# Attention's outputs kept as features by tokens in an adaLN transformer block

## The chip, the cores and the metric

The kernel runs on one core of a Trainium2 chip. A core has five engines with a queue each, which work through their instructions in order and wait for each other by semaphores: TensorE (PE in the profile, with its weight loads as PEld), VectorE (DVE), ScalarE (ACT), GpSimd (POOL) and SyncE (SP), which here only issues DMAs. The metric is the device time of one execution in microseconds (us), the median of several runs.

## The reference

An adaLN block over 2048 tokens of 576 features: 32 heads of 18 features, full softmax attention, then a gated layer of width 4608.

```python
h = layernorm(x) * (1 + ca) + sa
q, k, v = split(h @ wqkv)                      # 32 heads of 18
o = softmax(q @ k.T * 18**-0.5) @ v            # per head
x = x + ga * (o @ wo)
h = layernorm(x) * (1 + cb) + sb
x = x + gb * ((sigmoid(h @ w_gate) * (h @ w_up)) @ w_down)
```

The six vectors sa, ca, ga, sb, cb and gb come from silu(c) @ w_mod. Everything is float32; many products are taken as sums of high and low parts.

## The kernel before

The program first normalizes x and projects q, k and v, which go to DRAM split in high and low parts (qd, kd) or stay in SBUF (vaug). Then comes attention, and then the gated layer as a long row of products in which PE is filled to the brim.

Attention runs over 32 units: two halves of 1024 queries, and in each 16 pairs of heads. A unit has 16 steps kt, one for each 128 keys. A step does four score products (L1084: 128 keys by 512 queries, two heads by two blocks c of 512), four exponentials on ACT (L1088) and, two steps behind, the products of the exponentials with the values (L656). These add up over the unit in one PSUM tile `o` of 128 rows, in which head h and block c take the rows from 32 (2 h + c): 18 rows of outputs, features by queries, and below them a row of the exponentials' sums. Beside this each step computes a part of the row maxima for the units ahead (L550 on PE, L556, L559 and L561 on DVE and ACT).

The order on PE and ACT is written out by hand. A table `STEPS` has a line of words for each kind of pair of steps: `t` is a score product with its exponential, `m`, `r` and `x` a product for the maxima, `V` the values of a step, `A` and `B` their halves, `K` calls taken(), `G` asks the generator rows0 or rows1 for its next piece, and `c` moves every piece of work in the list `follow` one step on. A piece that ends with "g" makes the next pair of steps a heavy one, with the order "full"; the others take "half", "rows" (units 15 to 27) or a line of their own for kt 0, 2, 4 and 12. DVE, POOL and SP are ordered by a scheduler; an instruction given to paced() also waits for the exponential written last. bank() hands out seven PSUM banks in turn to the score products, the maxima and everything else in attention.

At a unit's start load_heads(u + 2) has SP issue eight loads of q and k (L514 to L522, 1512 KB). Where a unit's maxima are complete, spread() turns them and SP issues four small DMAs from mrows into the q tile (L590), about at kt 12.

A unit's end, before: taken() copies `o` to oT in SBUF (L673, at kt 1 of the next unit). At kt 2, outputs() turns oT back to tokens by features with four transposes on PE (L683), ACT copies the result (L699), DVE takes the reciprocals of the sums (L702), GpSimd scales (L705) into Os[half], 1024 tokens by 576 features in SBUF. The projection by wo then works row tile by row tile (project_o): three or four transposes of a row tile (L772), one more for the last 64 features in the first half (L789), copies on DVE (L774 to L790), splits on GpSimd, and two groups of products (L805). Row tiles 0 to 7 run in units 16 to 20, row tiles 8 to 15 in units 27 to 31 over the first 384 features only; the other 192 features go through DRAM (oend) and are added in last_rows(), during the gated layer, again with transposes (16).

Of the kernel before, what the change touches and what calls it, by code (L numbers as in the profile page):

```python
# [23 lines left out]
P = 128  # L24
# [63 lines left out]
def tile_block(ctx, tc, x_in, wqkv, wo, w_gate, w_up, w_down, c_in, w_mod, out):  # L88
# [206 lines left out]
    oend = dram.tile([P, 8, D - DL], F32, name="oend")  # L295
# [338 lines left out]
    Os = [Oa]  # L634
# [33 lines left out]
    def taken():  # L668

        if "whole" in state:  # L670
            half, p, acc = state.pop("whole")
            oT = epool.tile([P, 512], F32, name="oT")
            nc.scalar.copy(oT, acc)  # L673
            state["end"] = (half, p, oT)

    def outputs():

        if "end" not in state:
            return
        half, p, oT = state.pop("end")  # L680
        tp = bank().rearrange("p (b q) -> p b q", q=P)
        for b in range(4):
            nc.tensor.transpose(tp[:, b, :], oT[:, b * P : (b + 1) * P], ident)  # L683

        yield
        tq = tp.rearrange("p b (j e) -> p j b e", e=32)
        rec = epool.tile([P, 4, 4], F32, name="rec")
        if half == 1 and p == H // 2 - 1:
            nc.vector.reciprocal(rec, tq[:, :, :, DH])
            state["last"] = epool.tile([P, 512], F32, name="oT")[:, 0 : 16 * DH].rearrange("p (t e) -> p t e", t=8)  # L690
            for h in range(2):
                nc.vector.tensor_tensor(
                    state["last"][:, :, h * DH : (h + 1) * DH].rearrange("p (c b) e -> p c b e", c=2),
                    tq[:, 2 * h : 2 * h + 2, :, 0:DH],
                    rec[:, 2 * h : 2 * h + 2, :].unsqueeze(3).to_broadcast([P, 2, 4, DH]),
                    op=ALU.mult,
                )
            return
        nc.scalar.copy(oT, tp.rearrange("p b q -> p (b q)"))  # L699
        yield  # L700
        tq = oT.rearrange("p (b j e) -> p j b e", j=4, e=32)
        nc.vector.reciprocal(rec, tq[:, :, :, DH])  # L702
        for h in range(2):
            f0 = (2 * p + h) * DH
            nc.gpsimd.tensor_tensor(  # L705
                Os[half][:, :, f0 : f0 + DH].rearrange("p (c b) e -> p c b e", c=2),
                tq[:, 2 * h : 2 * h + 2, :, 0:DH],
                rec[:, 2 * h : 2 * h + 2, :].unsqueeze(3).to_broadcast([P, 2, 4, DH]),
                op=ALU.mult,
            )  # L710


# [4 lines left out]
    def load_wo():  # L717
# [31 lines left out]
        for _ in range(4):  # L749
            yield  # L750
# [3 lines left out]
    def project_o(t):  # L754

        wo_h, wo_l, we = weights
        if t <= 8:
            held_rows[:] = temp([P, 2048], F32R), temp([P, 2048], F32)
        T, T_ = held_rows
        if t < 8:  # L760
            xt, full, od = T_[:, 0:D], T_[:, 1024:1536], T_[:, 1536:1664]
        else:
            T, T_ = T[:, 1024 * (t % 2) : 1024 * (t % 2) + 1024], T_[:, 960 * (t % 2) : 960 * (t % 2) + 960]
            xt, full = T_[:, 0:D], T_[:, D : D + 384]
        nc.gpsimd.dma_start(xt, x_rows[:, t, :])
        src = Os[t // 8][:, t % 8, :]
        n = 4 if t < 8 else DL // P
        oh = T[:, 0 : n * P]
        ol = T[:, 512 : 512 + n * P]
        pt = bank()  # L770
        for i in range(n):
            nc.tensor.transpose(pt[:, i * P : (i + 1) * P], src[:, i * P : (i + 1) * P], ident)  # L772
# [1045 lines left out]
```

## Time and profile before

| what | value |
|---|---|
| median of 3 runs | 2798.32 us (2797.94 to 2798.35) |
| the profiled execution: its time, its span | 2804.88 us, 2803.1 us |
| mean granted clock of TensorE | 0.998 |
| busy: PE, DVE, ACT, POOL | 2771.9, 2306.3, 1609.3, 814.6 us |
| attention | from about 236 to 1533 us |
| a unit without projection work | 38.3 us |

The profile is one execution. Its page gives busy times of the engines, the chain of work that ended last, groups of equal instructions (a count, the mean time of one, and what the engine waited for before it) and the DMA issues; the trace behind it can be asked for a stretch of time or one engine. A row of a timeline has start, length, engine, source line, operation and tiles, and in brackets the idle time before it and who ended that. Matmuls overlap, so the distance between starts tells more than the length of one.

### The profile page before, as it was taken

Reading aid. Unit: us, or ns where it says so; the run is one execution under the profiler, and the core shown is the slowest. Engines: PE = TensorE matmul, PEld = TensorE weight load, DVE = VectorE, ACT = ScalarE, POOL = GpSimd, SP = SyncE. Lnnn points to the kernel's source line nnn. Section 1 sums busy time; section 2 is a strip of 40 time slices with the busy share of each in tenths; the row PEclk is TensorE's granted clock in tenths of the full one; section 3 lists DMA queues with packets and bytes.
Section 4 is the critical chain, followed back from the end, with each engine's and each line's share of the span. In section 5 each row is a group of like instructions: output and inputs, shape, how many; then the busy total and the mean of one; then the engine's idle time right before and its main releaser. Section 6 shows DMA issues by size and latency. Waiting matters only on the chain.

```text
span 2803.1 us, 50644 instructions
## 1 busy us (share of the span) xinstructions
PE 2771.9 (99%) x18637; PEld 1847.4 (66%) x18637; DVE 2306.3 (82%) x4370; ACT 1609.3 (57%) x3051; POOL 814.6 (29%) x1077
## 2 busy tenths in 40 slices
PE   7999999999999999999999999999999999999999
PEld 5975444444444444444444888888888888888888
DVE  7278999999998888999883778888898677777777
ACT  3215999999999878999888332333333222222221
POOL 3125207888843111663103222232221100000000
PEclk9999999999999999999999999999999999999999
DMA  5344224444432120232127766667767956566653
GB/s 172 121 157 140 78 61 162 171 169 166 172 133 82 36 58 24 98 106 71 43 68 227 273 222 223 240 213 273 278 245 280 339 195 201 194 200 195 200 195 120
DMA packets 170777, 462.59 MB, mean 165 GB/s; under 512 B 21212, under 2 KB 88032, under 8 KB 160416
## 3 DMA queue, kind: packets, MB, share of 16 engines
q1 hardware_dynamic: 150064, 360.72, 38.4%
q0 software_dynamic: 20464, 98.62, 9.9%
q8 instruction: 147, 2.41, 0.4%
q14 instruction: 102, 0.84, 0.1%
HBM read 281.92 MB, written 176.82 MB: 164 GB/s over the span
## 4 chain that ended last, share of the span: by engine, by line
PE 92%; DVE 4%; DMA 2%; issue 2%; POOL 0%; ACT 0%; SPq 0%; DVEq 0%; ACTq 0%; POOLq 0%
PE x L1225 26%; PE o L656 19%; PE s L1084 12%; PE s L550 11%; PE d L1375 8%; PE d L1307 6%; PE s L336 4%; PE s L805 2%; PE s L389 1%; DMA out_dram<-Oa 1%; DVE mx L556 1%; PE s L683 1%; DMA wq_raw<-in_A_wqkv_dram 1%; DVE w L1215 0%; DVE Oa L1379 0%
## 5 line engine op out<-in xcount | busy, mean ns | idle before, releaser
L1088 ACT ACTIVATE p<-s 128x512 f32<-128x512 f32 x2048 | 1069.1, 616 | 89.2 <-PE s L1084 62.6
L556 DVE TENSOR_REDUCE mx<-s 128x1 f32<-128x512 f32 x1568 | 1000.9, 683 | 101.3 <-PE s L550 75.1
L656 PE MATMUL o<-p,vaug 128*32 128x256 f32 (+1 forms) x5848 | 595.1, 478 | 0.1
L550 PE MATMUL s<-k,q 54*128 54x512 f32 x1920 | 548.6, 434 | 2.0 <-DVE t L775 1.0
L1084 PE MATMUL s<-q,k 56*128 56x512 f32 x1920 | 527.7, 440 | 0.0
L550 PEld LDWEIGHTS s<-k,q 54*128 54x128 f32 x1920 | 273.4, 184 | 231.9 <-DVE mx L561 88.0
L1084 PEld LDWEIGHTS s<-q,k 56*128 56x128 f32 x1920 | 249.8, 184 | 232.1 <-ACT p L1088 72.9
L1225 PE MATMUL x<-k,w 128*128 128x512 f32 x1512 | 370.0, 392 | 0.0
L1225 PEld LDWEIGHTS x<-k,w 128*128 128x128 f32 x1512 | 276.8, 188 | 53.3 <-PE o L656 0.8
L1375 PE MATMUL d<-wd,hh 128*128 128x288 f32 x1248 | 249.9, 295 | 2.4 <-DVE Oa L1379 2.4
L656 PEld LDWEIGHTS o<-p,vaug 128*32 128x32 f32 x5848 | 116.2, 108 | 203.1 <-issue 187.5
L1225 PE MATMUL x<-big,w 128*128 128x512 f32 x1008 | 245.5, 392 | 0.7 <-DVE u L1724 0.7
L1225 PE MATMUL x<-w,w 128*128 128x512 f32 x1008 | 245.3, 391 | 0.0
L1225 PEld LDWEIGHTS x<-big,w 128*128 128x128 f32 x1008 | 185.1, 188 | 37.0 <-DVE u L1724 1.1
L1225 PEld LDWEIGHTS x<-w,w 128*128 128x128 f32 x1008 | 184.3, 188 | 34.5
L1375 PEld LDWEIGHTS d<-wd,hh 128*128 128x128 f32 x1248 | 202.2, 188 | 6.2 <-DVE Oa L1379 3.1
L1375 PE MATMUL d<-wd,hl 128*128 128x288 f32 x624 | 184.3, 295 | 0.0
L1379 DVE TENSOR_TENSOR Oa<-Oa,d 128x288 f32<-128x288 f32 x312 | 136.6, 453 | 55.1 <-PE d L1375 51.2
L561 DVE CUSTOM_DVE_ANT_0 over<-s,over 128x512 f32<-128x512 f32 x240 | 163.9, 683 | 1.3 <-PE s L1084 1.2
L559 ACT ACTIVATE over<-s 128x512 f32<-128x512 f32 x240 | 145.8, 608 | 11.3 <-PE s L550 9.3
L1234 ACT ACTIVATE sg<-x 128x512 f32<-128x512 f32 x36 | 21.6, 599 | 210.2 <-PE x L1225 210.2
L1206 ACT CAST w<-S 128x768 fp32r<-128x768 f32 x71 | 59.4, 836 | 137.8 <-POOL S L1179 136.0
(275 smaller groups left out, 3898.5 us busy)
## 6 DMA issues: line engine op xcount, KB each, us to landing
ws<-w SPq DMA_DIRECT2D x126, 640.0 KB
w<-ws SPq DMA_DIRECT2D x126, 640.0 KB
wd<-wds SPq DMA_DIRECT2D x19, 1152.0 KB
k<-kd SPq DMA_DIRECT2D x60, 360.0 KB
wds<-w POOLq DMA_DIRECT2D x18, 1152.0 KB, 5.2
wtd<-t POOLq DMA_DIRECT2D x32, 576.0 KB, 5.0
wt<-wtd SPq DMA_DIRECT2D x64, 288.0 KB
wd<-wds SPq DMA_DIRECT2D x52, 288.0 KB
```

The lines of the kernel that those rows point to most:

```text
L336: nc.tensor.matmul(acc, w, hT[:, t, cols], start=n == 0, stop=n == len(ts_) - 1)
L550: nc.tensor.matmul(sp, qs[rows, qt * P : (qt + 1) * P], ks[rows, at * 512 : (at + 1) * 512], start=True, stop=True,)
L556: nc.vector.tensor_reduce(to, sp, axis=AX.X, op=ALU.max)
L559: nc.scalar.activation(over, sp, AF.Relu)
L561: nc.vector.tensor_tensor_reduce(out=over, in0=sp, in1=over, scale=1.0, scalar=LOWEST, op0=ALU.add, op1=ALU.max, accum_out=mx[:, h * n + q ...
L656: nc.tensor.matmul(acc[32 * j : 32 * j + 32, cols], vaug[:, kt, (2 * p + h) * VW : (2 * p + h) * VW + 32], probs[2 * c + h][:, cols], star ...
L1084: nc.tensor.matmul(sT, ks[rows, kcols], qs[rows, c * 512 : (c + 1) * 512], start=True, stop=True)
L1088: state["exp"] = nc.scalar.activation(pr, sT, AF.Exp, scale=SCALE)
L1225: nc.tensor.matmul(acc[v], w[:, v, a, :], X[s][:, b, :], start=first and n == 0, stop=n == 6, skip_group_check=not first,)
L1307: nc.tensor.matmul(acc, a[:, rows], w[:, k, :], start=n == 0, stop=n == 2)
L1375: nc.tensor.matmul(acc[:, :HALF], a[:, f, rows], w[:, f, cols], start=n == 0, stop=n == 5)
L1379: nc.vector.tensor_add(Oa[:, t, cols], Oa[:, t, cols], acc[:, :HALF])
```

## The change

The outputs stay features by tokens. After the copy of `o` to oT, four DMAs lay the four rows of sums over the partitions of sT (each row of 512 over 32 partitions of 16). DVE inverts them in one instruction, a DMA writes them to DRAM (osums), and another reads each row back over 32 partitions into R. GpSimd multiplies oT by R, and four DMAs store the scaled rows in `ot` in DRAM, 576 features by 2048 tokens. outputs() is now a generator in `follow`: the reciprocal comes at the first `c` with kt of 2 or more, the multiply at the first with kt of 6 or more.

The projection reads `ot` back into SBUF (load_rows, in five or three pieces, at set units) and GpSimd splits the columns of a row tile (rows_parts) one row tile ahead; project_rows has the products alone, as pieces that are all heavy. The hold of heavy pieces at kt 2 is gone, and so are the lines of STEPS for kt 2 and 4. The last unit's `o` goes to DRAM unscaled (lastd), and last_rows() inverts its sums, reads the rest from `ot` and needs no transposes; there DVE multiplies by R instead.

The diff, cut to its core (in the rows further down that are of the changed program, line numbers are those of the changed file):

```diff
@@ STEPS
-    2: "V m1t0 t1t0 m0m1 O A c m1r0 t1m0 t1t0 G B c x0t1 m1t0",
-    4: "V r0m1 t1t0 m1m0 G A c t0t1 m1t0 B t1m0 m1t0 t1x0",
@@ taken(), outputs()
+        oT = epool.tile([P, 512], F32, name="oT")
+        nc.scalar.copy(oT, acc)
+        if half == 1 and p == H // 2 - 1:
+            nc.sync.dma_start(lastd, oT)
+            return
+        sT = epool.tile([P, 16], F32, name="sT")
+        for j in range(4):
+            one = oT[32 * j + DH : 32 * j + DH + 1, :]
+            nc.sync.dma_start(sT[32 * j : 32 * j + 32, :], one.rearrange("l (q r) -> l q r", r=16))
+        follow.append(outputs(half, p, oT, sT))
...
-        for b in range(4):
-            nc.tensor.transpose(tp[:, b, :], oT[:, b * P : (b + 1) * P], ident)
...
-        nc.scalar.copy(oT, tp.rearrange("p b q -> p (b q)"))
...
-        nc.vector.reciprocal(rec, tq[:, :, :, DH])
...
+    def outputs(half, p, oT, sT):
+        while state["kt"] < 2:
+            yield
+        rec = epool.tile([P, 16], F32, name="rec")
+        paced(nc.vector.reciprocal(rec, sT))
+        to = osums[half * H // 2 + p]
+        nc.sync.dma_start(to.rearrange("j (q r) -> (j q) r", r=16), rec)
+        R = state["room"] if "room" in state else bgp.tile([P, 512], F32, name="R")
+        nc.sync.dma_start(R, to.unsqueeze(1).to_broadcast([4, 32, 512]))
         yield
+        while state["kt"] < 6:
+            yield
+        paced(nc.gpsimd.tensor_mul(oT, oT, R))
+        for h in range(2):
+            for c in range(2):
+                f0, n0, j = (2 * p + h) * DH, half * HW + c * 512, 2 * h + c
+                nc.sync.dma_start(ot[f0 : f0 + DH, n0 : n0 + 512], oT[32 * j : 32 * j + DH, :])
@@ the projection
+        nc.gpsimd.dma_start(xt, x_rows[:, t, :])
+        src = state["rows"][:, 0:n, cols]
...
+        nc.gpsimd.tensor_copy(oh3, src)
+        nc.gpsimd.tensor_sub(ol3, src, oh3.bitcast(F32))
...
-            nc.tensor.transpose(pt[:, i * P : (i + 1) * P], src[:, i * P : (i + 1) * P], ident)
...
+                if h == 0 and t < t0 + 7:
+                    ahead = rows_parts(t + 1)
...
+                yield "g" if t < t0 + 7 or h == 0 else None
@@ the loop over units
-                hold = heavy and (kt == 2 or kt == 12 and u < UNITS - 1)
+                hold = heavy and kt == 12 and u < UNITS - 1
```

Three places in the built programs show what moved. First SP, from the start of one unit (its loads for two units on) to the start of the next, in the middle of attention. Before:

```order
L514 DMA q_1025<-qd 36x1x1024
L517 DMA q_1025<-qd 18x1024
L518 DMA k_2233<-kd 36x1x2560
L522 DMA k_2233<-kd 18x2560
L514 DMA q_1025<-qd 36x1x1024
L517 DMA q_1025<-qd 18x1024
L518 DMA k_2233<-kd 36x1x2560
L522 DMA k_2233<-kd 18x2560
L590 DMA q_1029<-mrows 1x8x128 x4
L514 DMA q_1021<-qd 36x1x1024
```

With the change, the same place:

```order
L514 DMA q_1031<-qd 36x1x1024
L517 DMA q_1031<-qd 18x1024
L518 DMA k_2232<-kd 36x1x2560
L522 DMA k_2232<-kd 18x2560
L680 DMA sT<-oT 32x1x16 x4
L690 DMA osums<-rec 128x16
L692 DMA R<-osums 128x1x512
L700 DMA ot<-oT 18x512 x4
L590 DMA q_1023<-mrows 1x8x128 x4
L514 DMA q_1027<-qd 36x1x1024
```

Ten DMAs stand between the loads of the heads and those from mrows now: four to sT, one to osums, one to R, four to `ot`. (The second list begins at the second half of the eight loads.)

Second, DVE around the reciprocal of a unit in the middle of attention. L556 reduces one score tile, L561 (two rows) folds a pair of them. Before:

```order
L561 ISA mx_1040 128x1
L556 TENSOR_REDUCE mx_1040<-s_7218 128x1
L556 TENSOR_REDUCE mx_1040<-s_7235 128x1
L556 TENSOR_REDUCE mx_1040<-s_7250 128x1
L556 TENSOR_REDUCE mx_1040<-s_7253 128x1
L702 RECIPROCAL rec<-oT 128x16
L556 TENSOR_REDUCE mx_1040<-s_7267 128x1
```

With the change:

```order
L561 ISA mx_1042 128x1
L556 TENSOR_REDUCE mx_1042<-s_7503 128x1
L556 TENSOR_REDUCE mx_1042<-s_7514 128x1
L556 TENSOR_REDUCE mx_1042<-s_7525 128x1
L556 TENSOR_REDUCE mx_1042<-s_7528 128x1
L688 RECIPROCAL rec<-sT 128x16
L556 TENSOR_REDUCE mx_1042<-s_7539 128x1
```

The reciprocal kept its place, behind the third reduce of kt 2; its operand is sT in place of the copied transposes.

Third, PE at the same kt 2 before the change, between the first score products and the halves of the values:

```order
L1084 MATMUL s_7246<-q_1029,k_2230 128x512
L550 MATMUL s_7250<-k_2233,q_1025 128x512
L550 MATMUL s_7253<-k_2233,q_1025 128x512
L683 MATMUL s_7256<-ident,oT 128x128 x4
L656 MATMUL o<-p_7212,vaug 32x256
```

With the change the row L683 is gone there, in all units, and so are the 64 transposes of the projection and 16 of last_rows(); the products of the projection are the same in number and shape.

More of the change, by code (lines that the diff above doesn't have):

```diff
@@ L876, in first_rows @@
         yield from load_wo()
-        for t in range(8):
-            yield from project_o(t)
+        yield from project_rows(0)
         for t in range(8):
@@ L995, in down_parts @@
                     yield
-    def last_rows_project():
-        for t in range(8, NT):
-            yield from project_o(t)
     def load_block(pool, b, k, tied=None):
@@ L1133, in tile_block @@
     taken()
-    for _ in outputs():
-        pass
     manual.close()
-    nc.sync.dma_start(oend[:, :, D - DL - 2 * DH :], state["last"])
     att.close()
```

210 lines of the change are left out of this document (97 added, 113 removed).

## Prediction

> **What bounds the kernel now.** I read the page's first rows and its chain first, then attention by stretches of time, then single units on each engine.
>
> ```profile
> span 2803.1 us, 50644 instructions
> PE 2771.9 (99%) x18637; PEld 1847.4 (66%) x18637; DVE 2306.3 (82%) x4370; ACT 1609.3 (57%) x3051; POOL 814.6 (29%) x1077
> PE 92%; DVE 4%; DMA 2%; issue 2%; POOL 0%; ACT 0%; SPq 0%; DVEq 0%; ACTq 0%; POOLq 0%
> ```
>
> TensorE is nearly always busy and holds the chain. So work taken off it pays in full, and a wait that stops it costs in full. Two stretches of attention, by engine (PE, PEld, DVE, ACT, POOL busy, then the granted clock, the DMA share and GB/s):
>
> ```profile
> 636.00:716.00 80.00, 80.00 (x686) 34.70 (x682) 74.07 (x140) 78.05 (x157) 60.01 (x97) 1.00 0.49 175
> 1280.00:1360.00 80.00, 80.00 (x670) 33.05 (x668) 72.72 (x139) 76.45 (x154) 7.34 (x11) 1.00 0.18 54
> ```
>
> PE never idles there; ACT (78.05 of 80) and DVE (74.07) have little room. The second stretch has little GpSimd work and little DMA; the first has GpSimd preparing the down weights, with 175 GB/s. Unit 27 lies in the quiet stretch; I use it as the pattern. Its pair of steps kt 2, 3 on PE, ACT and DVE:
>
> ```profile
> 1326.36 1.07 PE L656 MATMUL o<-p,vaug 128*32 128x512 f32 x8
> 1328.34 0.66 PE L683 MATMUL s<-ident,oT 128*128 128x128 f32 x4
> 1328.92 0.64 PE L656 MATMUL o<-p,vaug 128*32 128x256 f32 x8
> 1331.70 1.07 PE L656 MATMUL o<-p,vaug 128*32 128x512 f32 x8
> ...
> 1325.68 0.62 ACT L673 COPY oT<-o 128x512 f32<-128x512 f32 x1
> 1329.50 0.73 ACT L699 COPY oT<-s 128x512 f32<-128x512 f32 x1
> ...
> 1327.89 1.89 DVE L556 TENSOR_REDUCE mx<-s 128x1 f32<-128x512 f32 x3 [0.41 <-PE s L550]
> 1330.33 0.25 DVE L702 RECIPROCAL rec<-oT 128x16 f32<-128x16 f32 x1 [0.55 <-ACT oT L699]
> ```
>
> The four transposes hold PE from 1328.34 to 1328.92: **0.58 us**. The pair runs from 1326.36 to 1331.70.
>
> **What the change takes away.**
>
> ```profile
> L683 PE MATMUL s<-ident,oT 128*128 128x128 f32 x128 | 20.9, 286 | 0.1
> L772 PE MATMUL s<-ident,Oa 128*128 128x128 f32 x32 | 5.2, 287 | 0.2
> ```
>
> Of the 128 transposes of oT, 31 fours lie in the units and one at the end; a four is 0.58 us, so one is 0.145. The projection loses 64 transposes (40 for the first eight row tiles, 24 for the second), 64 x 0.145 = 9.3 us, and the last rows 16, 2.3 us. ACT loses 31 copies (L699), DVE the copies of L774, L778 and L790. The matmuls of L805 stay 368.
>
> ```profile
> L705 POOL TENSOR_TENSOR Oa<-oT,rec 128x144 f32<-128x144 f32 x32 | 13.1, 431 | 97.8 <-DVE rec L702 97.6
> L848 POOL TENSOR_TENSOR t<-t,t 128x512 fp32r<-128x512 f32 x9 | 11.6, 1285 | 0.3
> ```
>
> GpSimd's two multiplies of 0.43 us a unit become one of about 1.29. GpSimd has 20 us to spare in 80, and nobody waits for the product before the next unit's copy into oT, some 30 us on; should GpSimd come that late, ACT and with it PE would wait. Of the new DMAs behind the reciprocal (osums, R, four to ot), only SP is held; behind them on SP stand the mrows DMAs, needed some 25 us later. I cost them at nothing. The removed hold at kt 2 only moves heavy pairs of steps; their number, 16 in each half, stays.
>
> **What it adds.** The reciprocal stays at the same place of DVE's order, behind the third reduce of kt 2, but now waits for four small DMAs (sT) in place of an ACT copy. SP issues them behind the loads of the heads two units on. SP in unit 27, and one row for the cost of a small issue:
>
> ```profile
> 1321.51 1.65 SPq L514 DMA_DIRECT2D q<-qd  x2
> 1326.24 0.49 SPq L522 DMA_DIRECT2D k<-kd  x1
> L590 SPq DMA_DIRECT2D q<-mrows x128: 620/630/1506, 216.5 to 1491.0; - x128
> ```
>
> The copy of oT ends at 1325.68 + 0.62 = 1326.30, SP is free at 1326.73, and four issues of 0.63 end at about 1329.3. By then the bytes of the eight loads are still in flight. One unit moves 2 x (360 + 180 + 144 + 72) = 1512 KB. Quiet unit 27, every 2 us:
>
> ```profile
> 1324.00:1326.00 2.00, 2.00 (x22) 1.05 (x18) 2.00 (x4) 2.00 (x5) 0.00 (x0) 1.00 0.59 175
> 1326.00:1328.00 2.00, 2.00 (x18) 0.68 (x16) 1.59 (x5) 2.00 (x5) 0.00 (x0) 1.00 0.49 179
> 1328.00:1330.00 2.00, 2.00 (x20) 0.90 (x18) 1.78 (x3) 2.00 (x5) 0.00 (x0) 1.00 0.57 160
> 1330.00:1332.00 2.00, 2.00 (x20) 0.80 (x22) 1.67 (x4) 1.97 (x5) 0.82 (x2) 1.00 0.60 184
> 1332.00:1334.00 2.00, 2.00 (x22) 0.65 (x14) 1.70 (x5) 2.00 (x5) 0.00 (x0) 1.00 0.07 20
> ```
>
> The stream drains at about 1332.2, 5.5 us after SP's last issue, at 160 to 184 GB/s. Does a small transfer pass it on the same queue? Unit 2 answers:
>
> ```profile
> 324.50 0.41 SPq L126 DMA_DIRECT2D big<-in_w_mod_dram  x1
> 325.06 0.51 SPq L198 DMA_DIRECT2D gates<-w  x2
> 330.54 0.35 SPq L199 DMA_DIRECT2D ga_b<-gates  x1
> x1p<-t POOLq DMA_DIRECT2D x8, 288.0 KB, 2.4
> ```
>
> Two writes of 1.1 KB stood behind a load of 1152 KB; the read that needs them left only at 330.54, 5.0 us after their issue ended, where 288 KB with nothing ahead land in 2.4. So a small transfer waits its turn. The Trainium skill, "DMA: Bandwidth & Descriptors", section "Queues, rings and completion order", says that each DMA engine takes a queue's descriptors in ring order; this trace agrees. Its section on why a DMA increments its semaphore by 16 puts a copy on the lowest-numbered engines; by that the sums share the loads' engines; no row here names an engine.
>
> So sT lands about 2 us behind the drain, near **1334.2**. DVE arrives at the reciprocal at 1327.89 + 1.89 = 1329.78 and stands for 4.4 us. Every reduce is queued behind it. PE hands out seven PSUM banks in turn; after `c` the eighth score of the order "rows" wants the bank of the first reduce that DVE owes. Without the transposes that pair would end at 1331.70 - 0.58 = 1331.12, and PE stops one pair of matmuls (0.34) before, at 1330.8. It goes on when DVE has done the reciprocal (0.25) and one reduce (0.69, three in 1.89): 1335.1. The next V starts at about 1335.5 where it started at 1331.70: **+3.8 us**, the removed transposes counted in. Nothing gives it back, since PE had no idle time to shed.
>
> Units 5 to 14 share the DMA engines with GpSimd's 175 GB/s. In unit 12, which lies 620.2 us earlier (oT's copy at 705.50), the stream is not down at the same distance:
>
> ```profile
> 705.50 0.63 ACT L673 COPY oT<-o 128x512 f32<-128x512 f32 x1
> 714.00:716.00 2.00, 2.00 (x22) 0.99 (x18) 1.79 (x4) 2.00 (x5) 0.00 (x0) 1.00 0.58 234
> ```
>
> There I take +6.0, the drain some 2 us later (estimate; GpSimd's own transfers are in that row too). For the 13 quiet units (3, 4, 15, 16, 19 to 27) I take 4.2. In 17, 18, 28 and 29 kt 2 becomes a heavy "full" pair, `c` comes some 3 us later, and about +0.5 is left. In 1, 2, 30 and 31 little or nothing is queued ahead: -0.3.
>
> **The clock.** PE would idle 4 to 6 us in each of 23 units. The trace has one stall at the start of attention:
>
> ```profile
> 237.41 0.50 PE L1084 MATMUL s<-q,t 56*128 56x512 f32 x1 [0.94 <-DVE pl L343]
> 236.00:240.00 4.00, 2.96 (x18) 1.17 (x20) 3.93 (x7) 3.72 (x9) 0.00 (x0) 0.89 0.81 219
> 240.00:244.00 4.00, 4.00 (x18) 1.16 (x22) 2.88 (x6) 1.88 (x5) 2.00 (x3) 0.50 1.05 342
> 244.00:248.00 4.00, 4.00 (x22) 1.58 (x18) 2.45 (x5) 2.14 (x6) 3.89 (x4) 0.76 0.74 243
> 243.37 1.93 PE L656 MATMUL o<-p,vaug 128*32 128x512 f32 x8
> 247.62 1.07 PE L656 MATMUL o<-p,vaug 128*32 128x512 f32 x8
> ```
>
> After 0.94 us of idle the granted clock fell to 0.50, and the same eight matmuls took 1.93 in place of 1.07. The lost share is 4 x (0.11 + 0.50 + 0.24) = 3.4 us of PE work. A longer stall should trip it too, but part of the slow time then falls into the stall. Bounds 0 and 3.4; I take 2.5, nearer the row. The Trainium skill, "TensorE: Matmul & The Clock Gate", Part 1, says that the clock halves after an idle window of about 3.4 us and returns after a busy one; the rows agree in kind, though less idle sufficed here. An estimate by that page is 1.7 to 3.4 per stall.
>
> **Sum, against the profiled execution** (span 2803.1, its time 2804.88; the median shown, 2798.32, is 6.6 lower, and I carry the difference over): 13 x 4.2 + 10 x 6.0 = 115; 4 x 0.5 - 4 x 0.3 = +1; clock 23 x 2.5 = 58; projection -9.3, last rows -2.3, the end -0.6, and +1 for DVE's two extra multiplies in the last rows. Together +162 us: 2805 + 162 = 2967 profiled, **2960** as a median.
>
> **Rivals.**
> - *The stall without the clock.* If PE's other work keeps the gate open, the 58 falls away: 2798 + 104 = 2902. Against it stands the row at 237.41.
> - *The sums are not held by the loads* (they run on engines of their own, or small packets pass). Then only issue counts: last issue from 1328.6, landing about 2 us on, 1330.6 against DVE's 1329.78: 0.8 us, of which the banks cover most. Gain of a unit about 0.2: -31 x 0.2 - 11 = 2781, **faster**. It decides where sT lands before about 1331. Unit 2's gates speak against it.
> - *DVE is late anyway and nothing waits*: the full 31 x 0.58 + 11 = 29: 2769. DVE's idle of 0.41 and 0.55 just there speaks against it.
> - *A standstill within 0.2%* needs the wait to cost just what the transposes gave, some 1 us a unit: possible only if the sums land between the two cases.
>
> **Chances.** Forecast with the clock 0.62, stall without it 0.20, sums not held 0.08, full gain 0.07, balance 0.03. Faster by over 0.2% 0.15, within 0.2% (about what a measurement of this kernel can tell from no change) 0.03, slower 0.82. The ends: 23 units at 3.8 without the clock and the gains give 2798 + 87 - 12 = 2873, at 6.5 with 3.4 each 2798 + 228 - 11 = 3015; I set 2850 to 3040, and leave the 0.18 of the faster cases out.
>
> **What would show it.** Right: the reciprocal of sT idles 4 to 6 us and names a DMA; PE idles after it in 23 units; PEclk below 1.0 all through attention; chain shares for DMA and DVE rise; u 30 and 31 run as before. Wrong: reciprocals that wait under 1 us, or PE at 80 of 80 in the two stretches. If PE stalls at a clock of 1.00, only the 58 was wrong.

## The result, and the profile after

| what | before | after |
|---|---|---|
| median | 2798.13 us, 4 runs (2795.52 to 2798.35) | 2840.78 us, 4 runs (2838.20 to 2846.87) |
| ratio after to before | | 1.0158, 95% interval 1.0138 to 1.0177 |
| profiled execution: time, span | 2804.88, 2803.1 us | 2838.20, 2836.4 us |
| mean granted clock of TensorE | 0.998 | 0.987 |

The change costs 43 us. The direction was predicted; the forecast of 2960 us was 119 too high, and 2840.78 lies under the range of 2850 to 3040.

From the page of the kernel after: span, busy engines, the chain that ended last, and the group of score products, whose last column is TensorE's idle time before them.

```profile
span 2836.4 us, 50932 instructions
...
PE 2766.0 (98%) x18429; PEld 1834.5 (65%) x18429; DVE 2291.9 (81%) x4342; ACT 1595.7 (56%) x3020; POOL 830.9 (29%) x1048
...
PE 84%; DMA 7%; DVE 3%; POOL 2%; issue 2%; SPq 1%; ACT 0%; POOLq 0%; DVEq 0%; ACTq 0%
...
L1072 PE MATMUL s<-q,k 56*128 56x512 f32 x1920 | 544.4, 446 | 39.6 <-DMA q<-mrows 32.9
```

PE is busy 5.9 us less than before and the span is 33.3 longer. (That is 33 and not 43 because the profiled execution before took 6.75 us more than its median and the one after 2.6 less; the comparisons of traces below go by the 33.3.) The chain has gone from 92% PE to 84%, and DMA from 2% to 7%. The wait has a name, but not the predicted one: of 39.6 us ahead of the score products, 32.9 are a wait for `q<-mrows`, the DMAs of which the prediction said that they are "needed some 25 us later". The wait that was predicted, DVE's for sT, is there once. The waits of the whole of attention, kernel after (us in total, times, longest):

```profile
PE s L1072 <- DMA q<-mrows: 32.9, 12, 11.9
...
PE s L1072 <- DVE mx L556: 5.8, 3, 4.1
...
DVE rec L688 <- DMA sT<-oT: 4.1, 1, 4.1
```

The stretches of the kernel after that answer to the two of before (us, busy engines, then granted clock, DMA share, GB/s), and those in which the clock fell:

```profile
640.00:684.00 44.00, 39.82 (x323) 16.66 (x324) 35.91 (x67) 37.37 (x74) 32.65 (x51) 0.95 0.46 156
1247.00:1327.00 80.00, 80.00 (x680) 32.72 (x676) 74.25 (x143) 77.69 (x158) 20.43 (x22) 1.00 0.29 89
236.00:1568.00 1332.00, 1288.81 (x10320) 549.85 (x10317) 1130.94 (x2150) 1179.98 (x2351) 595.93 (x811) 0.97 0.35 116
430.00:860.00 430.00, 408.77 (x3304) 170.14 (x3296) 368.12 (x690) 383.57 (x762) 305.47 (x473) 0.95 0.49 169
860.00:910.00 50.00, 38.11 (x311) 15.36 (x307) 33.93 (x64) 35.22 (x72) 27.10 (x31) 0.86 0.38 114
1480.00:1536.00 56.00, 51.89 (x395) 20.31 (x391) 35.79 (x69) 46.04 (x93) 17.26 (x23) 0.94 0.45 132
```

The quiet stretch runs at 80 of 80 and a clock of 1.00. The loss lies in 430 to 910 us (units 5 to 15) and in unit 30. Attention as a whole, by the first and last start of its exponentials, after and then before:

```profile
L1076 ACT ACTIVATE p<-s x2048: 570/605/752, 235.9 to 1567.6; 128x512 f32<-128x512 f32 x187
```

```profile
L1088 ACT ACTIVATE p<-s x2048: 570/604/765, 236.1 to 1531.2; 128x512 f32<-128x512 f32 x187
236.00:1532.00 1296.00, 1291.84 (x10510) 561.51 (x10509) 1144.28 (x2178) 1194.45 (x2382) 580.47 (x842) 1.00 0.32 106
```

That is 1331.7 us against 1295.1, +36.6; the rest of the program is 3.3 shorter (33.3 - 36.6). By the first exponentials of the units, units 5 to 14 alone take 419.0 us (431.48 to 850.49) where they took 383.1 (435.33 to 818.43): 35.9 of the 36.6. There GpSimd prepares the down weights. PE's idle time in attention went from 4.2 (1296 - 1291.84) to 43.2 us, +39.0. The half clock took 0.05 x 430 + 0.14 x 50 + 0.06 x 56 = 32 us, a part of it inside the idle time.

### Where the reciprocal really stands

In the quiet unit 25, from its first exponential to the next unit's, ACT and then DVE of the kernel after:

```profile
1284.92 2.11 ACT L1076 ACTIVATE p<-s 128x512 f32<-128x512 f32 x4
...
1322.79 1.62 ACT L1076 ACTIVATE p<-s 128x512 f32<-128x512 f32 x3
```

```profile
1303.32 1.89 DVE L556 TENSOR_REDUCE mx<-s 128x1 f32<-128x512 f32 x3 [0.37 <-PE s L550]
1305.12 0.24 DVE L688 RECIPROCAL rec<-sT 128x16 f32<-128x16 f32 x1
```

The reciprocal starts 20.2 us into a unit of 37.87, in kt 8, and waits for nothing. So the sentence above on the change, that it kept its place behind the third reduce of kt 2, is wrong: the rows shown there for the changed kernel are those of kt 8. They look alike (four reduces behind an L561) because each pair of steps has the same pattern. The scheduler that orders DVE put the reciprocal off to kt 8 or so in units 3 to 29. Of the units with reduces beside it, it stands earlier in three, in which SP issues fewer or none of the eight head loads ahead of sT: at kt 4 in unit 1 (five ahead), and at kt 2 in unit 2 (the four of q) and in unit 30 (none). The scheduler's estimate cannot be seen; that it counts these loads is inferred from those three units.

### What the late reciprocal holds up

SP in unit 10 (first exponential at 640.44), from the sums on; then POOL and PE:

```profile
644.53 3.23 SPq L680 DMA_DIRECT2D sT<-oT  x4
662.62 0.36 SPq L690 DMA_DIRECT2D osums<-rec  x1
664.06 0.60 SPq L692 DMA_DIRECT2D R<-osums  x1
676.37 1.69 SPq L700 DMA_DIRECT2D ot<-oT  x4
678.16 3.99 SPq L590 DMA_DIRECT2D q<-mrows  x4
```

```profile
674.29 0.80 POOL L981 TENSOR_TENSOR t<-t 128x288 fp32r<-128x288 f32 x1
675.06 1.28 POOL L696 TENSOR_TENSOR oT<-oT,R 128x512 f32<-128x512 f32 x1
```

```profile
683.50 1.16 PE L1072 MATMUL s<-q,k 56*128 56x512 f32 x2 [4.18 <-DMA q<-mrows]
```

Read upwards from PE: the first score of unit 11 waits 4.18 us for mrows. Its DMAs went out at 678.16, because SP takes its work in order and stood at the `ot` stores until 676.37. The stores waited for GpSimd's multiply (675.06), which was queued behind the work on the down weights and needs R, whose load left at 664.06 after a reciprocal at kt 8. In the quiet units GpSimd is free, the stores are out in time, and nothing waits. SP's waits in the kernel after from 400 to 1400 us:

```profile
SPq L690 <- DVE rec L688: 328.9, 24, 15.9
SPq L700 <- POOL oT L696: 197.3, 24, 18.1
```

Two places differ. In unit 15 the multiply stood behind the projection's weights, which GpSimd loads through two buffers; PE then waited 11.9 us, the longest wait of the table:

```profile
888.21 1.39 POOL L726 TENSOR_TENSOR t<-t,ga_b 128x576 f32<-128x576 f32 x1 [3.07 <-DMA t<-in_A_wo_dram]
...
890.28 1.26 POOL L696 TENSOR_TENSOR oT<-oT,R 128x512 f32<-128x512 f32 x1
```

And in unit 30, where the reciprocal does stand at kt 2, the waits that the prediction described are seen, on DVE and then on PE:

```profile
1504.75 0.25 DVE L688 RECIPROCAL rec<-sT 128x16 f32<-128x16 f32 x1 [4.14 <-DMA sT<-oT]
```

```profile
1505.61 0.79 PE L1072 MATMUL s<-q,k 56*128 56x512 f32 x1 [4.11 <-DVE mx L556]
...
1506.33 1.93 PE L655 MATMUL o<-p,vaug 128*32 128x512 f32 x8
```

What made sT late there is not what the prediction named. No head loads stand ahead of it; SP's last issue for sT ends at 1498.77, and sT is there only some 6 us later, where it takes 1.2 us in unit 25 of e10 (a run told of below), with nothing large ahead and little on the DMA engines. GpSimd's own queue was moving 1280 KB pieces of xs at that time, and kept the DMA engines full:

```profile
1502.00:1504.00 2.00, 0.00 (x0) 0.00 (x0) 0.00 (x0) 0.66 (x2) 0.00 (x0) 1.00 1.09 429
```

That these transfers held the small ones of another queue is inferred from their times; no run moves them.

### The profile page after: what moved, and what is told of

Same layout as the page of the kernel before. It is cut to its first block, busy times and chain, and to the rows that moved or that the text cites. A ratio compares the mean times of both kernels' runs of the same rounds, so it can differ in the third digit from the quotient of the medians.

```text
span 2836.4 us, 50932 instructions
## 1 busy us (share of the span) xinstructions
PE 2766.0 (98%) x18429; PEld 1834.5 (65%) x18429; DVE 2291.9 (81%) x4342; ACT 1595.7 (56%) x3020; POOL 830.9 (29%) x1048
## 4 chain that ended last, share of the span: by engine, by line
PE 84%; DMA 7%; DVE 3%; POOL 2%; issue 2%; SPq 1%; ACT 0%; POOLq 0%; DVEq 0%; ACTq 0%
PE x L1214 26%; PE o L655 17%; PE s L1072 11%; PE s L550 9%; PE d L1364 7%; PE d L1296 6%; PE s L336 4%; PE s L794 2%; PE s L389 1%; DMA q<-mrows 1%; DVE mx L556 1%; DMA out_dram<-Oa 1%; DMA wq_raw<-in_A_wqkv_dram 1%; DMA wds<-w 1%; DMA t<-in_A_wo_dram 0%
## 5 line engine op out<-in xcount | busy, mean ns | idle before, releaser
L556 DVE TENSOR_REDUCE mx<-s 128x1 f32<-128x512 f32 x1568 | 1003.5, 684 | 153.2 <-PE s L550 114.5
L655 PE MATMUL o<-p,vaug 128*32 128x256 f32 (+1 forms) x5848 | 604.9, 484 | 0.2 <-ACT oT L673 0.2
L1072 PE MATMUL s<-q,k 56*128 56x512 f32 x1920 | 544.4, 446 | 39.6 <-DMA q<-mrows 32.9
L550 PE MATMUL s<-k,q 54*128 54x512 f32 x1920 | 559.4, 442 | 0.0
L1072 PEld LDWEIGHTS s<-q,k 56*128 56x128 f32 x1920 | 256.8, 188 | 303.3 <-issue 93.2
L550 PEld LDWEIGHTS s<-k,q 54*128 54x128 f32 x1920 | 280.0, 188 | 212.8 <-DVE mx L561 67.1
L561 DVE CUSTOM_DVE_ANT_0 over<-s,over 128x512 f32<-128x512 f32 x240 | 164.0, 683 | 2.9 <-PE s L550 1.5
L1223 ACT ACTIVATE sg<-x 128x512 f32<-128x512 f32 x36 | 21.6, 599 | 207.0 <-PE x L1214 207.0
```

What stands on the lines that cost most here:

```text
L550: nc.tensor.matmul(sp, qs[rows, qt * P : (qt + 1) * P], ks[rows, at * 512 : (at + 1) * 512], start=True, stop=True,)
L556: nc.vector.tensor_reduce(to, sp, axis=AX.X, op=ALU.max)
L561: nc.vector.tensor_tensor_reduce(out=over, in0=sp, in1=over, scale=1.0, scalar=LOWEST, op0=ALU.add, op1=ALU.max, accum_out=mx[:, h * n + q ...
L655: nc.tensor.matmul(acc[32 * j : 32 * j + 32, cols], vaug[:, kt, (2 * p + h) * VW : (2 * p + h) * VW + 32], probs[2 * c + h][:, cols], star ...
L1072: nc.tensor.matmul(sT, ks[rows, kcols], qs[rows, c * 512 : (c + 1) * 512], start=True, stop=True)
```

## The experiments

Theory A: the loss comes from what waits in order on SP (and behind it) for a scaled output that is late. Theory B: the new DMAs crowd the DMA engines, so mrows lands late wherever it is issued. Theory C, the prediction's own: DVE waits for sT. All runs, with the waits of their profiled executions in attention (us; the kernel before took 2798 to 2800 us beside each of them):

| run | median us | ratio, 95% interval | DVE for sT | PE for a maximum's bank | PE for mrows |
|---|---|---|---|---|---|
| the changed kernel | 2840.78 | 1.0138 to 1.0177 | 4.1 | 5.8 | 32.9 |
| e1 stores on GpSimd's queue | 2834.73 | 1.0111 to 1.0145 | 12.4 | 7.6 | 28.3 |
| e6 and row loads paced | 2835.76 | 1.0114 to 1.0152 | 11.3 | 6.6 | 8.9 |
| e9 and the product into R | 2817.83 | 1.0053 to 1.0084 | 11.2 | 6.2 | 19.3 |
| e2 reciprocal pinned, kt 2 | 2995.81 | 1.0683 to 1.0718 | 87.9 | 146.2 | - |
| e3 reciprocal pinned, kt 4 | 2901.09 | 1.0350 to 1.0381 | 14.7 | 64.3 | - |
| e5 order as written, kt 2 | 2982.07 | 1.0635 to 1.0676 | 153.8 | 141.1 | - |
| e4 order as written, kt 4 | 2850.16 | 1.0159 to 1.0207 | 48.3 | 47.5 | - |
| e7 order as written, kt 6 | 2811.90 | 1.0032 to 1.0063 | 6.0 | 5.8 | 20.1 |
| e10 e5, head loads behind sT | 2865.62 | 1.0223 to 1.0254 | 23.1 | 20.3 | 37.3 |
| e11 e10 with e9's edits | 2832.79 | 1.0107 to 1.0137 | 25.1 | 21.6 | 17.4 |
| e8 e7 with e9's edits | 2798.99 | 0.9995 to 1.0015 | 12.8 | 12.1 | 0.9 |
| e12 e8, loads paced | 2824.04 | 1.0081 to 1.0110 | 6.4 | 7.3 | 15.2 |
| e13 e8, units 14 and 16 mended | 2792.00 | 0.9961 to 0.9981 | 5.2 | 7.0 | 1.6 |

### The stores off SP's queue (e1), and two theories on DVE's place (e2, e3)

```diff
-                nc.sync.dma_start(ot[f0 : f0 + DH, n0 : n0 + 512], oT[32 * j : 32 * j + DH, :])
+                nc.gpsimd.dma_start(ot[f0 : f0 + DH, n0 : n0 + 512], oT[32 * j : 32 * j + DH, :])
```

> Edit: the four ot stores of each unit go out on GpSimd's queue instead of SP's; nothing else. Theory A (the SP queue: the mrows DMAs of the next unit stand behind the ot stores, which wait for R and for GpSimd's multiply): mrows is issued as soon as its own sub is done, so the score that waits for q<-mrows goes away in units 5 to 15 (39.6 us of waits on that line in the changed kernel), the clock is halved there no more, and the time falls to 2775 to 2795 us; what is left over is units 27 to 30. Theory B (contention: the small new DMAs fill the DMA engines, mrows lands late wherever it is issued): the DMAs are the same ones, so the score still waits for mrows and the time stays at 2830 to 2850. Theory C (the reciprocal holds DVE): DVE's order is the same, so the time stays at 2830 to 2850.

It took 2834.73 us, which is what theories B and C had it at, and 40 over theory A. SP's waits in this run, 400 to 900 us, show why:

```profile
SPq L690 <- DVE rec L688: 159.1, 12, 16.8
SPq L747 <- DMA ot<-oT: 62.2, 4, 23.8
```

SP no longer stands at the stores. It stands at L747, the loads that read the rows back, which are written at unit 14 and which the scheduler had put up to ten units ahead (one at 588.90 us, in unit 8); they wait for the very stores that had been taken off the queue. (Its wait at L690 for the reciprocal is over before the mrows DMAs are due.) The blocker had been replaced, so this run did not tell A from B.

e2 and e3 force the reciprocal ahead of the next reduce that is written after it (kt 2 and kt 4):

```diff
+                if "pin" in state and not (paired and kc == 0):
+                    tc.add_manual_dep(
+                        reduced.ins, state.pop("pin").ins.name,
...
-        paced(nc.vector.reciprocal(rec, sT))
+        state["pin"] = nc.vector.reciprocal(rec, sT)
+        paced(state["pin"])
```

> Edit: the next reduce that is written after the reciprocal is made to come after it, so that the scheduler cannot put it off; the reciprocal then stands at kt 3.25 to 3.75 of its unit in DVE's order instead of kt 8.25 to 8.75, about where the prediction had it. The prediction's mechanism: sT lands 10.3 us or more after the unit's start, DVE would be there at about 8, so the reciprocal waits 2 to 4 us with DVE idle in some 25 units, PE runs out of PSUM banks and the clock is halved behind each: 2860 to 2960 us, over the changed kernel. Theory A: the reciprocal comes earlier, so R, the multiply and the ot stores do too, and mrows is no longer held on SP: those 39.6 us go; if DVE's wait is short enough for the seven banks to cover it, 2775 to 2800 us, and if not, the loss moves from the unit's end to its kt 3 to 5.

> Edit: as the pinned one, but the reciprocal is asked for at kt 4 instead of kt 2, and stands at kt 5.25 to 5.75 (about 12.5 us after the unit's start), behind the landing of sT (10.3 us and later) and 7 us before its place in the changed kernel. Theory A: no wait of DVE, R lands at about 20 us, the multiply and the ot stores are done by 25 us, before mrows is due at 28 to 30: both stalls are gone, 2770 to 2790 us, with units 5 to 14 at 37.6 to 38 us. Theory B (contention): mrows still lands late, 2830 to 2850. The prediction's mechanism: no idle of DVE here but where sT lands later than 12.5 us.

2995.81 and 2901.09 us: the first goes the way of the prediction's mechanism, 36 over its range, and the second is 111 over theory A and 51 over theory B, though DVE waited for sT only 14.7 us. The built program of e3 explains it; DVE around a reciprocal, rows in their order:

```
L556 TENSOR_REDUCE mx0_1041<-s2_4227 128x1
L561 ISA over_4210,mx0_1041<-s4_4234,over_4210 128x512
L561 ISA mx0_1041 128x1
L694 RECIPROCAL rec_4203<-sT_4077 128x16
L556 TENSOR_REDUCE mx0_1041<-s6_4212 128x1
```

By its number, PE writes s_4212 before s_4227 and s_4234. The scheduler kept the reciprocal behind these and put off the one reduce tied to it, so a PSUM bank was held while PE came round to it: PE waits 64.3 us for a maximum's bank, more than four times what DVE waits for sT. The pin had an effect of its own, and both runs overstate the cost of the place.

### The order as written (e5, e4, e7), and the row loads paced (e6)

```diff
+    def behind(ins):
+        if "chain" in state:
+            tc.add_manual_dep(ins.ins, state["chain"].ins.name, ...)   # order only, no semaphore
+        state["chain"] = ins
...
+                if not (paired and kc == 0):
+                    behind(reduced)
...
+        inverted = nc.vector.reciprocal(rec, sT)
+        behind(inverted)
+        paced(inverted)
```

> Edit: every reduce of the maxima is held to the order written (no semaphore, only the order on DVE), and the reciprocal is one link of that chain, so it stands where it is written: at kt 2.75 (2.25 in units 15 to 27), which is exactly the place that the prediction gave it. In the pinned kernel the reduce behind the reciprocal had been put off by the scheduler, so a bank of PSUM was held too long beside the wait; here it is not. The prediction's mechanism: DVE stands at about 7 us after the unit's start until sT lands at 10.3 us and later, PE runs out of banks, the clock is halved behind each stall: 2900 to 3000 us, 4 to 10 us more in nearly every unit, all of it in kt 2 to 5, and kt 14 to 15 without loss. Rival (the wait is covered by the banks, and the pinned kernel's loss came from the reduce put off): 2770 to 2800.

2982.07 us, inside the range that the prediction's mechanism had been given. With the reciprocal at the place that the prediction assumed, its story is there line by line. Unit 24 (from 1353.44 us) of this run, DVE, then PE, then a stretch and the whole of attention:

```profile
1357.62 1.89 DVE L566 TENSOR_REDUCE mx<-s 128x1 f32<-128x512 f32 x3 [0.42 <-PE s L560]
1365.28 0.25 DVE L700 RECIPROCAL rec<-sT 128x16 f32<-128x16 f32 x1 [5.78 <-DMA sT<-oT]
```

```profile
1366.13 0.79 PE L1086 MATMUL s<-q,k 56*128 56x512 f32 x1 [5.13 <-DVE mx L566]
1366.85 1.93 PE L667 MATMUL o<-p,vaug 128*32 128x512 f32 x8
```

```profile
1366.00:1370.00 4.00, 3.87 (x15) 1.31 (x15) 2.33 (x6) 1.02 (x2) 3.49 (x4) 0.50 0.35 120
236.00:1711.00 1475.00, 1330.55 (x10316) 558.28 (x10317) 1131.15 (x2149) 1180.42 (x2348) 596.09 (x811) 0.92 0.32 104
```

DVE stands 5.78 us at the reciprocal, PE 5.13 behind it, the clock is 0.50 for the next stretch and the eight matmuls of a V take 1.93 us. DVE waits 26 times, 5.9 us on average (153.8 / 26), PE 25 times, 5.6 (141.1 / 25); PE never waits for mrows.

> Edit: the same chain, with the reciprocal asked for at kt 4: it stands at kt 4.75 (4.25 in units 15 to 27), 10.5 to 11.5 us after the unit's start. sT has landed between 10.3 and 17.7 us in the kernels so far, so by the prediction's mechanism DVE waits only in the units with late head loads (5, 7, 8, 9, 11, 12, 14), 1 to 6 us each: 2800 to 2840. If the loss of 102 us with the pin at kt 4 came from the reduce that was put off, most of it goes, and this is well under 2870; if it came from the reciprocal's place itself, this stays at 2880 to 2910.

2850.16 us, 10 over the range and 51 under the pinned kernel, though DVE waits longer for sT here (48.3 us against 14.7): the pin's reordering had been worth those 51. DVE's wait is down to 12 times.

> Edit: the same chain, with the reciprocal asked for at kt 6 (kt 4 in units 15, 16 and 27, whose rows are read back at kt 7 and 9): it stands at kt 6.75, some 16 us after the start, behind every landing of sT but unit 8's. The prediction's mechanism is out: no wait of DVE. Theory A (the stores on SP): R lands at about 23 us instead of 26.5, so the stores are out before mrows is due at 29 us where GpSimd is free; where GpSimd has a backlog (units 5 to 14) mrows is still held. 2785 to 2815 us. If the reciprocal anywhere ahead of kt 8 costs DVE what the two pinned kernels lost, 2850 and more.

2811.90 us, as theory A had it: 29 us under the changed kernel with nothing altered but DVE's order (its reduces as written, and the reciprocal among them at kt 6, in units 15, 16 and 27 at kt 4). DVE's wait for sT is nearly gone (6.0 us), and PE's wait for mrows is down from 32.9 to 20.1: some 14 us in units 5 to 12, where GpSimd has its backlog, and 4.9 around the start of unit 31.

e6 goes back to the scheduler's place and takes e1 further; every load of rows waits for the exponential beside which it is written:

```diff
-                nc.sync.dma_start(state["rows"][:, i, :], ot[i * P : (i + 1) * P, own])
+                paced(nc.sync.dma_start(state["rows"][:, i, :], ot[i * P : (i + 1) * P, own]))
```

> Edit: the ot stores on GpSimd's queue as before, and the loads that read the rows back (big<-ot) are tied to the exp beside which they are written, so the scheduler can't issue them on SP 100 to 400 us early. With the stores moved alone, mrows still came late in six units, and SP was seen to stand at big<-ot, which waits for the very stores that had been taken off the queue (62 us in four waits). Theory A in its wider form (anything that waits on SP ahead of mrows holds it): with both off the queue mrows goes out at 29 to 30 us in units 5 to 14, those units take 37.6 us, and the time is 2785 to 2805, with unit 15 (GpSimd's order) and unit 30 (the reciprocal at kt 2.75) left. Theory B (contention of the new DMAs): nothing changes, 2825 to 2845.

2835.76 us, in theory B's range again; but again the wait had moved. Attention's waits in e6:

```profile
PE o L655 <- ACT oT L673: 20.9, 5, 7.7
...
ACT oT L673 <- DMA ot<-oT: 15.4, 3, 7.8
...
PE s L1072 <- DMA q<-mrows: 8.9, 2, 7.2
```

PE's wait for mrows is 8.9 us where it was 28.3: so those DMAs are not slow wherever they are issued, they had been held, and theory B falls. Now ACT's copy into oT waits until the stores out of the single oT tile have landed, and the products of the values wait for ACT.

### Three holds taken away (e9, e8), and the head loads behind the sums (e10, e11)

In e9 and e8 GpSimd's product goes into R, so that oT is free once it has been read; e9 keeps the scheduler's place, e8 has e7's order:

```diff
-        paced(nc.gpsimd.tensor_mul(oT, oT, R))
+        paced(nc.gpsimd.tensor_mul(R, oT, R))
```

> Edit: the changed kernel with the scheduler's own place of the reciprocal (kt 8), with stores on GpSimd's queue, row loads tied to their exp, and the product written into R. Theory A in full: units 5 to 14 at 37.6 us; left are unit 15 (GpSimd's multiply behind the projection's weights, about 12 us), 16, 27 and 30 (4 to 11 us): 2790 to 2805 us, and no clock halves between 440 and 830 us. Theory B (contention): 2825 to 2845 as before.

> Edit: the chain with the reciprocal at kt 6 (2812 us), and with it the ot stores on GpSimd's queue, the row loads tied to their exp, and GpSimd's product written into R instead of oT, so that oT is free after the multiply and not after its stores (in the run with the rows paced, units 6, 9, 13 and 15 waited for the copy into oT behind DMA ot<-oT, 3.7 to 7.8 us each). Theory A in its full form (GpSimd's late multiply holds the next unit in three ways: mrows behind the stores on SP, mrows behind the row loads on SP, and oT's single tile): units 5 to 14 take 37.6 us, sum of attention near 1285, 2765 to 2785 us. If a fourth way is left, 2800 or so.

e9: 2817.83 us, 23 under the changed kernel and 13 over the expected range; of its PE waits for mrows, 19.3 us, one of 17.4 is at the end of unit 15: the multiply stands behind the projection's weights again, the first row load on SP waits for its stores, and the mrows DMAs stand behind that load. e8: 2798.99 us, level with the kernel before and 14 over the expected range. With PE's wait for mrows at 0.9 us, what is left is sT again; unit 14 on SP, then DVE:

```profile
778.70 2.56 SPq L761 DMA_DIRECT2D big<-ot  x3
782.69 5.50 SPq L692 DMA_DIRECT2D sT<-oT  x4
```

```profile
797.00 0.25 DVE L700 RECIPROCAL rec<-sT 128x16 f32<-128x16 f32 x1 [6.17 <-DMA sT<-oT]
```

The sums were issued behind three row loads of 512 KB, and even a reciprocal at kt 6 is too early for them.

e10 tests the cause that the prediction gave for sT's lateness. It is e5 with one swap on SP: the sums first, then the eight head loads, each tied to an exponential of kt 2:

```diff
-        if 0 < u < UNITS - 2:
-            load_heads(u + 2)
...
+            if kt == 2 and 0 < u < UNITS - 2:
+                load_heads(u + 2, paced)
```

> Edit: as the kernel with the reciprocal in the chain at kt 2 (2982 us), but the eight head loads of the unit after next are issued on SP behind the four sT DMAs instead of ahead of them, tied to the exp of kt 2. Nothing else is changed, so DVE still meets the reciprocal at kt 2.75. The prediction's mechanism (sT is late because it stands behind the head loads, and DVE waits for it): sT lands at about 6.2 us, as it does in units 1 and 2, which load no heads; DVE waits no more, the stalls of kt 2 to 5 and the clock's halves go, and the time falls by 150 us or more, to 2785 to 2820, with what is left in units 5 to 14 (the stores on SP behind GpSimd's backlog) and perhaps a late head load. Rival (DVE's place at kt 2 is dear in itself, or the sums take 8 us to lay over rows whatever stands ahead): 2900 or more.

2865.62 us, 116 under e5 by the swap alone, though 46 over the range. The waits of attention in e10:

```profile
PE s L1086 <- DMA q<-mrows: 37.3, 12, 12.3
...
DVE rec L700 <- DMA sT<-oT: 23.1, 12, 6.3
PE s L1086 <- DVE mx L566: 20.3, 9, 6.2
```

DVE's wait for sT falls from 153.8 to 23.1 us, PE's behind it from 141.1 to 20.3. That is shown: the sums were late because the head loads were issued ahead of them (whether by the order of the queue or by sharing the DMA engines, this pair of runs does not tell). Of the 23.1 us, 11.5 are in units 30 and 31, which load no heads. The rest went elsewhere: osums and R now stand behind the head loads, the multiply is late again, and PE waits 37.3 us for mrows. The Trainium skill, "DMA: Bandwidth & Descriptors", section "Queues, rings and completion order", says that each DMA engine consumes a queue's descriptors in ring order; by that rule a small transfer behind 1512 KB waits its turn, and e5 beside e10 agrees.

> Edit: head loads behind sT, the reciprocal in the chain at kt 2, stores on GpSimd's queue, row loads tied to their exp, the product written into R. If the prediction's mechanism (DVE's wait for sT) and theory A (the late multiply) are all of the loss, nothing is left of it: 2762 to 2785 us, and the full gain of the transposes left out, some 25 us, is seen.

e11 has the edits of e10, e9 and e6 together. 2832.79 us, a clear miss, 48 over its range: 25.1 us of waits for sT and 17.4 for mrows were left. Moving all head loads behind the sums puts osums and R behind the head loads; it is no cure.

### The version that beats both (e12, e13)

e12, on top of e8:

```diff
-            load_rows(u // 26, range(3) if u == 14 else range(2))
+            if u in (14, 26) and kt == 8:
+                load_rows(u // 26, range(3) if u == 14 else range(2))
+            if kt == (2 if u in (15, 16, 27) else 0) and 0 < u < UNITS - 2:
+                load_heads(u + 2, paced)
```

> Edit: the kernel with the reciprocal at kt 6 and stores, rows and product off (2799 us), with the row loads of units 14 and 26 issued at kt 8 instead of at the unit's start, and with the head loads issued behind the sums in units 15, 16 and 27 alone, where the reciprocal stands at kt 4. In that kernel unit 14 took 45.7 us because sT stood behind three row loads and landed at 21 us, and unit 16 took 46.0 because sT landed at about 14 us. Theory (all that is left is a wait for sT behind larger loads): unit 14 goes to 37.7 us and unit 16 to about 41.9, 10 to 12 us less: 2785 to 2790 us, 0.3 to 0.5% under the kernel before. If the time stays at 2795 to 2800, something outside attention gives the gain back.

2824.04 us, 25 worse than e8 and 34 over the expected range. I had tied every head load to an exponential, also where none was to be moved, and PE waited 15.2 us for mrows and 9.2 for the copy into oT. That run changed more than it should have, and does not tell which of its edits cost the time. e13, again on top of e8, moves the loads in units 14 and 16 alone:

```diff
-            load_rows(u // 26, range(3) if u == 14 else range(2))
+            if u in (14, 26) and kt == (4 if u == 14 else 0):
+                load_rows(u // 26, range(3) if u == 14 else range(2))
+            if (u, kt) == (16, 2):
+                load_heads(u + 2, paced)
```

> Edit: the kernel with the reciprocal at kt 6 and stores, rows and product off (2799 us), with two moves of loads on SP and nothing else: in unit 14 the three row loads are issued behind the four sT DMAs (kt 4) instead of ahead of them, and in unit 16 alone the head loads too (kt 2). The run before tied every head load to an exp, which issued them all 2 us later and pushed sT and the next unit's work back with them; here only these two units are touched. Theory (what is left of the loss is sT behind larger loads): unit 14 goes from 45.7 to about 37.7 us and unit 16 from 46.0 to about 42: 2785 to 2791 us, 0.3 to 0.5% under the kernel before. If it stays at 2796 to 2802, the loss of these units moves elsewhere.

2792.00 us (10 runs beside 14 of the kernel before), ratio 0.9971, interval 0.9961 to 0.9981, 1 us over the expected range: the loss is gone and a small gain is left. From e8 to e13 unit 14 goes from 45.74 to 37.64 us and unit 16 from 46.04 to 39.28, but unit 15 from 39.09 to 45.09, where DVE now waits 3.5 us for sT. The page of e13:

```profile
span 2792.0 us, 50952 instructions
...
PE 2750.4 (99%) x18429; PEld 1834.6 (66%) x18429; DVE 2289.4 (82%) x4342; ACT 1591.8 (57%) x3020; POOL 895.8 (32%) x1172
```

PE's busy time is 21.5 us under that of the kernel before (2771.9), which is most of the work taken off it (part of the rest is lengthened by the half clock: the mean granted clock is 0.993 where it was 0.998). The medians show 6 of them and the spans of the two profiled executions 11, since some waits remain (the largest for a maximum's bank, 7.0 us in four).

## Why the prediction was wrong

**What the transposes give: right in kind.** A quiet unit of the kernel before, from its first exponential to the next unit's:

```profile
1285.45 1.13 ACT L1088 ACTIVATE p<-s 128x512 f32<-128x512 f32 x2
...
1323.72 1.13 ACT L1088 ACTIVATE p<-s 128x512 f32<-128x512 f32 x2
```

38.27 us, where the kernel after takes 37.87: 0.40, of 0.58 predicted. In the first half, where the pairs of steps have another order, unit 1 takes 37.65 us (277.36 to 315.01) where it took 38.26 (279.05 to 317.31): 0.61. With the projection's and the last rows' transposes, e13's 21.5 us less of busy PE stand against the 18 + 9.3 + 2.3 + 0.6 = 30 predicted.

**The step that failed** is, in the prediction's words, "The reciprocal stays at the same place of DVE's order, behind the third reduce of kt 2". It stands at kt 8, 20.2 us into the unit where the prediction had 6.1 (1329.78 in a unit that begins at 1323.72), and sT has long landed there. With it fell the 115 us of waits and the 58 of the clock, but for unit 30. e5, which puts it where the prediction had it, takes 2982 us: had the place been right, 2960 would have been 22 too low. The kernel is slower, as was forecast, but by another path than the forecast's: that the direction came out was luck.

**The terms behind that step, measured in e5.** sT behind the head loads: right (e10). DVE's stand of 4.4 us in a quiet unit: 5.78 in e5's unit 24, and 5.9 on average over 26 units, quiet or not. PE's stop: 23 predicted, 25 found. The clock: e5's attention is 1475.9 us by its exponentials (234.7 to 1710.6, as its trace gives them), 180.8 over before; PE's idle time there is 1475 - 1330.55 = 144.5, or 140 more than before; the other 40.6 and the gains (14 units at 0.61, 17 at 0.40, and the 9.3 that were predicted for the projection: 24.6, an estimate) make 65 us for the clock, where 58 was predicted. By the Trainium skill, "TensorE: Matmul & The Clock Gate", Part 1, the clock halves after an idle window; the row at 1366 to 1370, 0.50 behind 5.13 us of idle, agrees. In the kernel after much less was enough: 1.73 us of idle before 725.78, and a granted clock of 0.52 from 727 to 731.

**The second failed step**: "Of the new DMAs behind the reciprocal (osums, R, four to ot), only SP is held; behind them on SP stand the mrows DMAs, needed some 25 us later. I cost them at nothing." This hold is most of the 43 us: of the 43.2 us that PE idles in attention 32.9 are waits for mrows, e9, which takes holds away with the reciprocal still at kt 8, is 23 us faster than the changed kernel, and e8, which leaves 0.9 us of these waits, is level with the kernel before. 25 us is what the reciprocal at kt 2 would have left; 14 us later 11 are left, and R, GpSimd's queue and four stores need more than that wherever GpSimd has a backlog. The prediction had named the danger for ACT ("should GpSimd come that late") and did not price it for SP. The sum as it came out: idle time of PE in attention +39.0, less what the transposes gave (24.6 by the count above), plus what the half clock cost outside the idle time, and together +36.6; so of the clock's 32 us about 22 fell outside the idle time.

**What was to show it.** It did: the prediction named "reciprocals that wait under 1 us" as proof against it, and only one of the 31 waits for sT at all.

**What stays open.** How much of the remaining distance between e13's 6 us and the 21.5 of work saved could be had was not tried further; nor was any other estimate given to the scheduler in place of an order by hand.

## What to carry to other kernels

Where a scheduler orders an engine, find an instruction's place by counting from something fixed (the unit's first score, a step's number) and not by the look of the rows around it: repeated patterns look alike, and a new operand can move an instruction by 14 us. A queue that is taken in order passes one late result on to everything behind it, so a new chain of DMAs is priced by what it delays there, not by its own length; and when one blocker is taken away, look for the next on the same path before the theory is dropped (here stores, row loads and a single tile stood behind each other). A small transfer that something waits for is better issued ahead of large ones, but not by moving everything large behind it: in e10 osums and R got late instead.

## What the runs showed of the hardware

Idle time of TensorE of 0.6 to 4.2 us at a time was paid nearly twice: from 430 to 860 us of the kernel after, PE idles 21.2 us (430 - 408.77) and the clock of 0.95 takes another 21.5, a small part of it inside the idle time. With the pin, which puts a reduce behind later ones (one place is shown above), the kernel took 51 us more in e3 than in e4, with only 14.7 us of waits for sT in DVE's own rows: PSUM banks handed out in turn are a queue as much as an engine is. Four DMAs of 2 KB landed 1.2 us after their issue with nothing large ahead (unit 25 of e10), and some 6 us after it while another queue kept the DMA engines full (unit 30 of the kernel after).
